# A fused S4D convolution and linear attention: softmax scaled on one sign, spectrum blocks permuted, the plan's priorities and engine leanings renumbered

## The chip, the cores and the metric

The kernel runs on one core of a Trainium2 chip. Its time is the device time of one execution in microseconds; of several executions the median is given. One execution is taken by the hardware profiler, and all rows of the trace come from that one. Engines are named as in the profile: PE (TensorE), DVE (VectorE), ACT (ScalarE), POOL (GpSimd), SP (SyncE, whose queue issues the DMAs).

## The reference

Two independent halves are computed from different inputs and concatenated along the last axis. L = S = 2048 positions, D = 576 channels, 32 heads of 18.

```python
# A: S4D long convolution, 128 states per channel
dt = exp(log_dt); A = -exp(log_A_real) + 1j * A_imag
C = (C_real + 1j * C_imag) * dt[:, None]
P = exp((A * dt[:, None])[:, :, None] * arange(L))
K = 2.0 * einsum("dn,dnl->dl", C, P).real
y = irfft(rfft(u.T, 2L) * rfft(K, 2L), 2L)[:, :L].T + u * D_skip

# B: linear attention with a learned feature map, per head
q, k, v = x @ wqkv
phi_q = concat(softmax(q @ w_phi), softmax(-(q @ w_phi)))   # 36 features
phi_k = concat(softmax(k @ w_phi), softmax(-(k @ w_phi)))
kv = phi_k.T @ v;  z = sum_s phi_k
o = (phi_q @ kv) / (phi_q @ z + 1e-6)
b = o.reshape(S, D) @ wo
```

## The kernel before

The program is written as some thousands of operations with a cost each, and a planner (`Plan.run`) puts them in order for all five engines before anything is emitted. An operation belongs to a numbered unit of a stage (`pl.at("query", 5)`), and a table `WANT` holds one due time for each unit. At every step the planner looks, on each engine, at the operations whose inputs and buffers are free and takes the one with the earliest start, and among those that could start within 100 ns of the engine's end the one with the smallest due time. TensorE pays a penalty `STAY` in that order for a change of its tile mode, ScalarE 1300 ns for a change of its activation table. An operation with two possible engines (an eviction from PSUM: ScalarE or VectorE; a sum of two tiles in SBUF: GpSimd or VectorE) goes where the planner expects it to end first. Where TensorE is expected to wait before a fresh PSUM buffer, the planner puts filler matmuls on a tile of zeros (`emit`, line 202), which keep the clock up. Nothing is reordered on the chip: each engine goes through its list and waits on semaphores.

The stages are:

- *fold*, *key* (16 tiles of 128 positions): w_phi is multiplied into the key weights (line 462 loads them); a tile of x is split into two fp32r parts, `xh` and `xl`, and multiplied with both parts of the weights, 42 matmuls a tile; then the softmax, and a matmul that adds to `kvt`.
- *softmax* (line 526 on): per head the largest and the smallest value (533, 534), the values less the largest (`e[:, 0]`), smallest less largest (`rg`), and rg less `e[:, 0]` for the other sign, one exponential over both signs (541), the sums over a head's 18 (542, 64 sums), a reciprocal (543), and one multiplication of all 1152 values.
- *query* (16 tiles): the same gemm and softmax, transposes of `e` to `fT` (618), matmuls with `kvb` that give numerator and denominator, division (634, 635), transposes of the result (645, 646), the output gemm, the store of `ot`.
- *u* (16 units): the first half of the transform of u, stored to `ud` in DRAM in 64 blocks.
- *mags*, *par* (6 blocks), *group* (36): the filter's powers. Six blocks of parameters; for each group GpSimd builds integer phases by doubling (824), ScalarE takes sines (833 to 835) and exponentials (854), VectorE multiplies them (859 to 864), TensorE sums over the states. *kfirst* (4) transforms the filter and stores it to `kd`.
- *product* (16): a product takes four blocks of u's transform and their mirror images (`block`, `take`, four to five DMAs `ub<-dram`), transforms them, multiplies with the filter's blocks (`ac`, 8 multiplications; then two differences and two sums of 128x288, `ac<-ac`), transforms back and stores `zo` to `zd` in six DMAs (`put`). *last* (16 units) reads `zd`, does the last transform and stores.

The mirror image of block q lies in block 64 - q, so a product's upper blocks stand in falling order and one at a time; `place` and `block` sort them out.

## Time and profile before

| what | value |
|---|---|
| executions shown | 649.92, 646.87, 649.16 us; median 649.16 |
| the profiled execution | 647.51 us, of which the span is 645.7 |
| granted TensorE clock, mean | 0.982 |
| DMA | 104.03 MB, mean 161 GB/s, 55.8% of sixteen engines' time |

In 40 equal slices of the span, the busy tenths of each engine, and the DMA share, are:

```profile
PE   8999999999999878988999989889999999998996
...
DVE  6899999999999879998799999879997889698762
ACT  4599599987867978697959598759945333235331
POOL 0355556445415363471362463425200001010000
```

A digit is the busy share of one slice of 16 us, 9 being 90% or more. TensorE's rows hold the fillers too. ScalarE and GpSimd are busy in the first three quarters, where the filter is built, and little in the last.

### The profile page before, as it was taken

What the parts mean: (1) busy time and instruction counts of PE and PEld (TensorE: products, weight loads), DVE (VectorE), ACT (ScalarE), POOL (GpSimd) and SP (SyncE); (2) the same over time, 40 slices, a digit from 0 to 9 for tenths busy, and PEclk for the clock granted to TensorE, in tenths of its full rate; (3) what the DMA queues carried; (4) which work ended last, traced back from release to release, by engine and by line L of the source; (5) the groups of instructions that cost most, each with busy time, mean ns of one, the idle gap of its engine ahead of it and who ended that gap; (6) DMA issues with size and microseconds to landing.
All of it is one profiled execution on the core that took longest, in us unless ns stands there. A gap on an engine that the chain in (4) does not pass through costs nothing.

```text
span 645.7 us, 19223 instructions
## 1 busy us (share of the span) xinstructions
PE 593.6 (92%) x7774; PEld 467.2 (72%) x7774; DVE 567.4 (88%) x1211; ACT 431.5 (67%) x704; POOL 213.0 (33%) x362
## 2 busy tenths in 40 slices
PE   8999999999999878988999989889999999998996
PEld 5878878887877756866766655665776867776885
DVE  6899999999999879998799999879997889698762
ACT  4599599987867978697959598759945333235331
POOL 0355556445415363471362463425200001010000
PEclk9999999999999978979999899999999999999999
DMA  8668543241036212137665686786476877875575
GB/s 217 199 220 265 149 136 125 90 123 46 22 87 181 68 41 65 36 82 201 204 180 144 171 222 162 193 235 175 132 249 168 249 221 227 243 210 151 161 226 166
DMA packets 101662, 104.03 MB, mean 161 GB/s; under 512 B 12358, under 2 KB 90054, under 8 KB 101574
## 3 DMA queue, kind: packets, MB, share of 16 engines
q1 hardware_dynamic: 101574, 102.81, 55.8%
q8 instruction: 61, 1.00, 0.7%
q14 instruction: 27, 0.22, 0.1%
HBM read 63.63 MB, written 39.06 MB: 159 GB/s over the span
## 4 chain that ended last, share of the span: by engine, by line
PE 36%; DVE 36%; ACT 10%; DMA 7%; issue 5%; SPq 4%; POOL 1%; POOLq 0%; DVEq 0%; ACTq 0%
PE ps L408 32%; DVE E L860 4%; DVE cs L859 4%; DVE e L422 4%; DVE small L542 3%; DVE E L862 2%; PE ps L618 2%; DVE E L864 2%; DVE ac L426 2%; DVE small L533 2%; DMA xi<-in_xT_dram 2%; DVE small L534 2%; SPq L596 2%; PE ps L202 1%; ACT ps L854 1%
## 5 line engine op out<-in xcount | busy, mean ns | idle before, releaser
L408 PE MATMUL ps<-wh,xl 128*128 128x288 f32 (+2 forms) x448 | 140.7, 314 | 1.3 <-DVE xl L422 1.0
L408 PE MATMUL ps<-wh,xh 128*128 128x378 f32 (+2 forms) x400 | 133.7, 334 | 1.4 <-ACT zi L413 0.8
L408 PE MATMUL ps<-wl,xh 128*128 128x378 f32 (+2 forms) x400 | 128.3, 321 | 0.0
L824 POOL TENSOR_TENSOR cs<-cs,pi 128x32 int32<-128x32 int32 (+4 forms) x180 | 114.8, 638 | 12.8
L408 PEld LDWEIGHTS ps<-wh,xl 128*128 128x128 f32 x448 | 84.3, 188 | 2.4 <-DVE xl L422 1.6
L408 PEld LDWEIGHTS ps<-wh,xh 128*128 128x128 f32 x400 | 75.3, 188 | 10.0 <-issue 2.3
L408 PEld LDWEIGHTS ps<-wl,xh 128*128 128x128 f32 x400 | 75.3, 188 | 0.0
L408 PE MATMUL ps<-E,cs 128*32 128x64 f32 x2304 | 46.1, 229 | 18.5 <-DVE E L862 12.9
L202 PE MATMUL ps<-zero 128*32 128x256 bf16 (+10 forms) x310 | 56.5, 318 | 4.1 <-DVE E L860 1.4
L408 PEld LDWEIGHTS ps<-E,cs 128*32 128x32 f32 x2304 | 37.2, 115 | 31.5 <-DVE E L862 16.7
L854 ACT ACTIVATE ps<-ps 128x512 f32<-128x512 f32 x108 | 56.7, 584 | 4.3 <-PE ps L408 3.9
L426 DVE TENSOR_TENSOR ac<-us,ps 128x288 f32<-128x288 f32 x128 | 49.9, 441 | 2.6 <-PE ps L408 2.5
L422 POOL TENSOR_TENSOR xh<-xi,xh 64x128 fp32r<-64x128 f32 x21 | 11.5, 547 | 120.2 <-DVE small L543 60.9
L819 POOL MEMSET cs<- 128x16 f32 x36 | 4.8, 133 | 138.9 <-PE ps L408 108.4
L859 DVE TENSOR_TENSOR cs<-ps,cs 128x1024 f32<-128x1024 f32 x36 | 43.7, 1215 | 7.2 <-ACT ps L854 7.0
L202 PEld LDWEIGHTS <-zero 128*128 128x128 bf16 (+6 forms) x310 | 30.1, 105 | 26.2 <-issue 15.4
L541 ACT ACTIVATE e<-e 128x1152 f32<-128x1152 f32 x32 | 37.1, 1168 | 17.8 <-DVE e L422 16.5
L542 DVE TENSOR_REDUCE small<-e 128x64 f32<-128x1152 f32 x32 | 42.7, 1342 | 6.8 <-ACT e L541 6.8
L408 PE MATMUL ps<-wh,xi 128*128 128x288 f32 x160 | 48.6, 306 | 0.0
L422 POOL TENSOR_TENSOR xl<-xi,xh 128x512 fp32r<-128x512 f32 x19 | 24.6, 1297 | 67.4 <-ACT xh L416 67.4
L408 PE MATMUL ps<-wl,xi 128*128 128x288 f32 x160 | 46.8, 295 | 0.0
L860 DVE TENSOR_TENSOR E<-ps,cs 128x1024 f32<-128x1024 f32 x36 | 43.4, 1204 | 0.0
(141 smaller groups left out, 1373.8 us busy)
## 6 DMA issues: line engine op xcount, KB each, us to landing
xi<-in_xT_dram SPq DMA_DIRECT2D x32, 320.0 KB
dram<-zi SPq DMA_DIRECT2D x16, 576.0 KB
dram<-zi SPq DMA_DIRECT2D x32, 288.0 KB
kb<-dram SPq DMA_DIRECT2D x32, 288.0 KB
zi<-dram SPq DMA_DIRECT2D x16, 576.0 KB
ub<-dram SPq DMA_DIRECT2D x62, 144.0 KB
ub<-in_u_dram SPq DMA_DIRECT2D x16, 288.0 KB
out_dram<-ot SPq DMA_DIRECT2D x16, 288.0 KB
```

The source lines that it names most:

```text
L202: self.matmul(t[0:cols, 0:n], self.zero.t[0:rows, 0:cols], self.zero.t[0:rows, 0:n])
L408: pe.matmul(o, l, r, start=start, stop=stop, skip_group_check=skip)
L422: op(eng, [c_dve(n) if e == "dve" else c_pool(n) for e in eng], lambda e: (dve if e == "dve" else pool).tensor_tensor(dst(), a(), b(), op= ...
L426: op(eng, c_dve(n) if eng == "dve" else c_pool(n), lambda: e.tensor_tensor(dst(), a(), b(), op=alu), r=r, w=w, lock=eng == "pool" or not a ...
L533: op("dve", c_dve(DH * m), lambda: dve.tensor_reduce(mx.t, v(), axis=AX.X, op=ALU.max), r=[p], w=[mx])
L534: op("dve", c_dve(DH * m), lambda: dve.tensor_reduce(mn.t, v(), axis=AX.X, op=ALU.min), r=[p], w=[mn])
L541: op("act", c_act(1152), lambda: act.activation(e.t, e.t, AF.Exp), r=[e], w=[e], table="exp")
L542: op("dve", 1270, lambda: dve.tensor_reduce(sm.t, e.t, axis=AX.X, op=ALU.add), r=[e], w=[sm])
L824: op("pool", c_pool(2 * n * W), lambda n=n, j=j: pool.tensor_tensor(x()[:, :, :, n:2 * n], x()[:, :, :, 0:n], pi.t[:, j:j + 2, gs].bitcast ...
L854: op("act", c_act(512), lambda p=p: act.activation(p.t, p.t, AF.Exp), r=[p], w=[p], table="exp")
L859: op("dve", c_dve(64 * W), lambda: dve.tensor_tensor(F(), both(M.t), F(), op=ALU.mult), r=[M, cs], w=[cs])
L860: op("dve", c_dve(64 * W), lambda: dve.tensor_tensor(E.t[:, :, :, 32:64], both(up.t), cs.t[:, :, :, 0:32], op=ALU.mult), r=[up, cs], w=[E])
```

## The change

**Softmax.** The maximum is taken negated (`negate=True`), so that maximum and minimum of a head lie side by side in one tile of pairs, and smallest less largest becomes a sum over pairs, a reduction with one input. For a query tile only the second sign is scaled, by (sum of the first sign) / (sum of the second); the factor common to both signs then cancels in the division, and the 1e-6 is multiplied by the first sign's sums (`total`). Key tiles keep the full scaling.

**Spectrum blocks.** The constants `f1` and `f2` are permuted, so that the four blocks of a product and their four mirror images each stand together. `take`, `put`, `place` and `block` go; a product loads `ub` in two DMAs of 128 partitions and stores `zo` in two. The tables `fu` and `fi` become one, `ff`.

**The plan.** A new table `LEAD` gives each named part of a stage (`pl.step`) an offset to its due time. `LEAN_ACT` and `LEAN_POOL` are added to VectorE's expected end where an operation may go to it or to ScalarE, or to it or to GpSimd: the first is -488 ns, the second +413. `STAY`, the 100 ns of the choice (`NEAR`) and all of `WANT` have new values, and a few costs are raised.

**Buffers.** `tmp` and `at` of the parameters share the buffers of `dt` and `ax`, `total` is new with three, and `small` has 8 buffers, not 12.

```diff
+    q = np.arange(32)
+    at = q // 4 * 4 + q % 2 * 2 + q // 2 % 2
+    q = np.concatenate([q, (64 - q)[1:], [32]])
+    at = np.concatenate([at, 32 + at[1:], [32]])
+    row = np.zeros(128, int)
+    for r in range(2):
+        row[2 * at + r] = 2 * q + r
+    f1, f2 = f1[:, row], f2[row]
...
+    def step(self, name):
+        self.part = name
...
-        self.ops.append([eng, cost, fn, deps, bufs, self.now - early, table, busy, lock and eng, (self.unit, early), mode, fill[0] if fill else None, alt])
+        self.ops.append([eng, cost, fn, deps, bufs, self.now - early - LEAD.get(self.part, 0.0), table, busy, lock and eng, (self.unit, early, self.part), mode, fill[0] if fill else None, alt])
...
-                        s = first(e, t, ops[k][8])
+                        s, late = first(e, t, ops[k][8]), 0.0
                         if e == "act" and ops[k][6] and table and ops[k][6] != table:
-                            s += 1300.0
+                            s, late = s + 1300.0, TURNOVER
...
+                            lean = LEAN_ACT if "act" in (e, x if main else ops[k][0]) else LEAN_POOL
+                            a, b = a + lean * (e == "dve"), b + lean * (e != "dve")
...
-                        key = (s if s > at[e] + 100.0 else at[e], ops[k][5] + (STAY if e == "pe" and ops[k][10] != mode else 0.0), k)
+                        key = (s + late if s + late > at[e] + NEAR else at[e], ops[k][5] + (STAY if e == "pe" and ops[k][10] != mode else 0.0), k)
...
-STAY = 4.0
+STAY, TURNOVER, NEAR, LEAN_POOL, LEAN_ACT = 39.6166, 43.0853, 13.9405, 412.6640, -488.3109
...
-            mx, mn = B("small", [128, m]), B("small", [128, m])
-            op("dve", c_dve(DH * m), lambda: dve.tensor_reduce(mx.t, v(), axis=AX.X, op=ALU.max), r=[p], w=[mx])
-            op("dve", c_dve(DH * m), lambda: dve.tensor_reduce(mn.t, v(), axis=AX.X, op=ALU.min), r=[p], w=[mn])
-            tt("dve", lambda: e.t[:, 0, hs, :], v, lambda: mx.t[:, :, None].to_broadcast([128, m, DH]), ALU.subtract, [p, mx], [e], DH * m)
-            tt("dve", lambda: rg.t[:, hs], lambda: mn.t, lambda: mx.t, ALU.subtract, [mn, mx], [rg], m)
+            ends = B("small", [128, m, 2])
+            op("dve", c_dve(DH * m), lambda: dve.tensor_reduce(ends.t[:, :, 0], v(), axis=AX.X, op=ALU.max, negate=True), r=[p], w=[ends])
+            op("dve", c_dve(DH * m), lambda: dve.tensor_reduce(ends.t[:, :, 1], v(), axis=AX.X, op=ALU.min), r=[p], w=[ends])
+            tt("dve", lambda: e.t[:, 0, hs, :], v, lambda: ends.t[:, :, 0:1].to_broadcast([128, m, DH]), ALU.add, [p, ends], [e], DH * m)
+            op("dve", c_dve(2 * m), lambda: dve.tensor_reduce(rg.t[:, hs], ends.t, axis=AX.X, op=ALU.add), r=[ends], w=[rg])
...
+        both = B("small", [128, 32, 2])
+        op("dve", c_dve(32), lambda: dve.tensor_copy(both.t[:, :, 0], sm.t[:, :, 0]), r=[sm], w=[both], lock=True)
+        op("dve", 270, lambda: dve.reciprocal(both.t[:, :, 1], sm.t[:, :, 1]), r=[sm], w=[both])
+        op("dve", c_dve(64), lambda: dve.tensor_reduce(rg.t, both.t, axis=AX.X, op=ALU.mult), r=[both], w=[rg])
+        tt(("pool", "dve"), lambda: e.t[:, 1], lambda: e.t[:, 1], lambda: rg.t[:, :, None].to_broadcast([128, H, DH]), ALU.mult, [e, rg], [e], 576)
...
+            op("dve", c_dve(n), lambda: dve.scalar_tensor_tensor(
+                den.t[:, :n], sm.t[:, h0:h0 + n, 0], 1e-6, pn.t[:, :n, 18], op0=ALU.mult, op1=ALU.add), r=[pn, sm], w=[den])
...
+        ff = B("ff", [128, 512])
+        op("sp", c_dma(128 * 2048), lambda: sp.dma_start(ff.t, i["ff"][p]), r=[ud], w=[ff])
...
+        four = lambda z, par: z.t[32 * par + 4 * p:32 * par + 4 * p + 4].rearrange("(j r) s d -> (r s) j d", r=2)
         for par in range(2):
-            for r in range(2):
-                put(par, r)
+            op("sp", c_dma(128 * 2304, 1152), lambda par=par: sp.dma_start(four(zd[half], par), zo[par].t), r=[zo[par]], w=[zd[half]])
```

The new numbers move instructions on every engine. Three places show how. The first is the start of SyncE's list of DMAs, before:

```order
L757 DMA dt<-in_ldt_dram 128x96
L759 DMA th<-in_aim_dram 128x96
L759 DMA cre<-in_cre_dram 128x96
L759 DMA cim<-in_cim_dram 128x96
L458 DMA fT<-in_wphi_dram 128x630
L462 DMA e<-in_wkT_dram 126x640 x3
L462 DMA E<-in_wkT_dram 126x640
L462 DMA kvb<-in_wkT_dram 72x640
L449 DMA xi<-in_xT_dram 128x5x128
L449 DMA zi<-in_wv_dram 128x5x192 x2
```

and after (`wkT` is the key weight in five blocks, `wv` the value weight in three, `xT` a tile of x, `u` a tile of u):

```order
L716 DMA ub<-in_u_dram 128x576
L463 DMA zi<-in_wv_dram 128x5x192
L463 DMA e<-in_wv_dram 128x5x192
L472 DMA fT<-in_wphi_dram 128x630
L476 DMA e<-in_wkT_dram 126x640 x2
L476 DMA E<-in_wkT_dram 126x640
L476 DMA kvb<-in_wkT_dram 72x640
L791 DMA dt<-in_ldt_dram 128x96
L793 DMA th<-in_aim_dram 128x96
L793 DMA cre<-in_cre_dram 128x96
L793 DMA cim<-in_cim_dram 128x96
L463 DMA xi<-in_xT_dram 128x5x128
```

The first u tile and two thirds of wv moved to the front, and the parameters behind the key weights; the fifth block of the key weights stands four loads after the last row shown, and the last third of wv after the first two stores `gd<-cs` of the magnitudes.

The second place is VectorE's list in one of the last products, between its multiplications `ac<-us,ps` and what follows, before:

```order
L426 TENSOR_TENSOR ac<-us_8022,ps 128x288 x4
L426 TENSOR_TENSOR ac<-us_8023,ps 128x288
L422 TENSOR_TENSOR ac<-ac 128x288
L426 TENSOR_TENSOR ac<-us_8023,ps 128x288
L422 TENSOR_TENSOR ac<-ac 128x288
L426 TENSOR_TENSOR ac<-us_8023,ps 128x288 x2
L426 TENSOR_TENSOR small<-small 128x16
L422 TENSOR_TENSOR ac<-ac 128x288
L422 TENSOR_TENSOR e<-small,e 128x576
L422 TENSOR_TENSOR ac<-ac 128x288
```

and after:

```order
L440 TENSOR_TENSOR ac<-us_7933,ps 128x288 x4
L440 TENSOR_TENSOR ac<-us_7934,ps 128x288 x4
L547 TENSOR_REDUCE small<-ps 128x16
L436 TENSOR_TENSOR ac<-ac 128x288
L548 TENSOR_REDUCE small<-ps 128x16
L557 TENSOR_REDUCE total<-e 128x2x32
L440 TENSOR_TENSOR e<-ps,small 128x288
L427 COPY us_8122<-ps 128x288
```

One of the four sums and differences is left on VectorE. The others stand in the last rows of GpSimd's list after the change, which held four `ac<-ac` in all before:

```order
L436 TENSOR_TENSOR xl<-xi,xh 128x512
L436 TENSOR_TENSOR xh<-xi,xh 64x128
L436 TENSOR_TENSOR ac<-ac 128x288 x3
L436 TENSOR_TENSOR e<-e,small 128x576
L436 TENSOR_TENSOR ac<-ac 128x288 x17
L436 TENSOR_TENSOR xh<-xi,xh 64x128 x2
```

The third place is SyncE's list around one of the later products, before:

```order
L922 DMA fi<-in_fi_dram 128x256
L1005 DMA dram<-zo 64x2x288 x2
L1008 DMA dram<-zo 64x288 x4
L922 DMA fu<-in_fu_dram 128x256
L939 DMA ub<-dram 64x2x288 x4
L968 DMA kb<-dram 128x2x288
L966 DMA fk<-in_fk_dram 128x256
```

and after:

```order
L967 DMA ub<-dram 128x2x288 x2
L960 DMA ff<-in_ff_dram 128x512
L1026 DMA dram<-zo 128x2x288 x2
L990 DMA kb<-dram 128x2x288
L988 DMA fk<-in_fk_dram 128x256
```

Six stores and four loads of 64 partitions became two and two of 128, and the loads of the next product stand ahead of the stores of the one before.

More of the change, by code (lines that the diff above doesn't have):

```diff
@@ new lines @@
+    ident=[-39.703],
+    fold=[-3814.5703, -4514.447, 174.1103, 544.6624],
+    start=[726.2842],
+    key=[-2909.7917, -0.0799, 220.563, 157.8162, -225.5153, 173.04, -1241.6879, -109.3988, -338.4576, -175.3779,
+          -2318.8196, 176.0873, 249.8555, 251.9596, -231.4053, 99.8816],
+    kv=[85.5267],
+    query=[476.857, 1690.9897, 4431.7125, 751.3041, 2777.2337, 589.8585, 3194.9953, 2789.5574, 367.711, 1380.6418,
+          914.5124, 1423.5053, 2499.5972, 1377.3193, 2733.1361, 817.2673],
+    u=[-102.8226, -226.0234, -1433.3706, -445.0721, -485.8874, -1597.2828, 880.8324, -734.4783, 728.5016, 739.4667,
+          -177.0395, 249.377, -557.77, 773.8434, 166.2647, -5869.6701],
@@ L387 @@
+    kfirst=[-2069.12, -388.4536, -152.51, 676.399],
+    product=[580.2793, 583.4571, 524.945, 1019.1475, 645.2543, 381.769, 375.2706, 687.6813, 2038.1628, 2418.0025,
+          2088.0002, 1103.4417, 2475.9162, 1427.038, 1252.1902, 1625.8165],
+    last=[326.0515, 549.9183, 360.8347, 614.2391, 1189.7141, 171.5588, 558.2575, -103.0095, 1111.1706, 1441.7724,
+          1346.2631, 1230.7698, 2479.1252, 3727.1339, 1655.5831, 3612.5906],
 )
@@ L399, in tags @@
                 pl.tag(t, p, n, window)
[L401 to L402 removed]
+    tags({1: "zero ident w1 w3 hp dsk kvb fT wh wl ks E sel dt th cre cim ax ay mx mn fx ld ldc",
+          2: "xi xh xl v1 o ot pi mg ff ub kb zo us2 ac yo zi", 3: "e fk total", 4: "cs", 8: "small"})
     tags({8: "ps"}, space=PSUM, window=1000)
@@ L539, in softmax @@
         tt(("pool", "dve"), lambda: e.t[:, 1], lambda: rg.t[:, :, None].to_broadcast([128, H, DH]), lambda: e.t[:, 0],
-           ALU.subtract, [rg, e], [e], 540)
-        op("act", c_act(1152), lambda: act.activation(e.t, e.t, AF.Exp), r=[e], w=[e], table="exp")
-        op("dve", 1270, lambda: dve.tensor_reduce(sm.t, e.t, axis=AX.X, op=ALU.add), r=[e], w=[sm])
-        op("dve", 470, lambda: dve.reciprocal(sm.t, sm.t), r=[sm], w=[sm])
-        tt(eng, lambda: e.t, lambda: e.t, lambda: sm.t[:, :, :, None].to_broadcast([128, 2, H, DH]), ALU.mult, [e, sm], [e],
-           1100)
+           ALU.subtract, [rg, e], [e], 576)
+        op("act", c_act(1152) + 40, lambda: act.activation(e.t, e.t, AF.Exp), r=[e], w=[e], table="exp")
+        pl.step("q2" if total else "k2")
+        op("dve", 1270, lambda: dve.tensor_reduce(sm.t.rearrange("p h s -> p s h"), e.t, axis=AX.X, op=ALU.add), r=[e], w=[sm])
+        if not total:
+            op("dve", 470, lambda: dve.reciprocal(sm.t, sm.t), r=[sm], w=[sm])
+            tt(FLEX, lambda: e.t, lambda: e.t, lambda: sm.t.rearrange("p h s -> p s h")[:, :, :, None].to_broadcast([128, 2, H, DH]),
+               ALU.mult, [e, sm], [e], 1100)
+            return e
+        both = B("small", [128, 32, 2])
[3 more added lines that the diff above has]
+        tt(("pool", "dve"), lambda: e.t[:, 1], lambda: e.t[:, 1], lambda: rg.t[:, :, None].to_broadcast([128, H, DH]), ALU.mult, [e, rg], [e], 576)
         return e
@@ L607, in query_tile @@
         ps = gemm_halves(load_x(t), wqo, have_q, 0)
-        e = softmax([(ps[c], slice(16 * c, 16 * c + 16), lambda c=c: ps[c].t.rearrange("p (h f) -> p h f", f=DH)) for c in range(2)], FLEX)
+        pl.step("q1")
+        sm = B("total", [128, 32, 2])
+        e = softmax([(ps[c], slice(16 * c, 16 * c + 16), lambda c=c: ps[c].t.rearrange("p (h f) -> p h f", f=DH)) for c in range(2)], sm)
+        pl.step("q3")
         fT = B("fT", [126, 10, 128])
@@ L830, in waves @@
     def waves(cs):
+        pl.step("g1")
         def f():
@@ L999, in product @@
             copy("any", lambda c=c, j=j, par=par: zo[par].t[:, j], lambda c=c: pz[c].t, [pz[c]], [zo[par]], HD)
-        def put(par, r):
-            q = 4 * p + 2 * r
-            s = lambda: zo[par].t[64 * r:64 * r + 64]
-            if not par:
-                op("sp", c_dma(64 * 2304, 1152), lambda: sp.dma_start(zd[half].t[q:q + 2].rearrange("j s d -> s j d"), s()), r=[zo[0]], w=[zd[half]])
-            else:
-                for j in range(2):
-                    op("sp", c_dma(64 * 1152, 1152), lambda j=j: sp.dma_start(block(1, 2 * r + j, zd[half]), s()[:, j]), r=[zo[1]], w=[zd[half]])
         for par in range(2):
-            for r in range(2):
-                put(par, r)
+            op("sp", c_dma(128 * 2304, 1152), lambda par=par: sp.dma_start(four(zd[half], par), zo[par].t), r=[zo[par]], w=[zd[half]])
     for half in range(2):
```

105 lines of the change are left out of this document (44 added, 61 removed).

## The prediction

> **What bounds the kernel now.** I read the page's engine totals first, then its chain, then the busy time of each engine by stretch.
>
> ```profile
> span 645.7 us, 19223 instructions
> ...
> PE 593.6 (92%) x7774; PEld 467.2 (72%) x7774; DVE 567.4 (88%) x1211; ACT 431.5 (67%) x704; POOL 213.0 (33%) x362
> ...
> PE 36%; DVE 36%; ACT 10%; DMA 7%; issue 5%; SPq 4%; POOL 1%; POOLq 0%; DVEq 0%; ACTq 0%
> ```
>
> No one engine owns the end: PE and DVE have equal shares of the chain of waits. An average over the span hides which of them leads where, so I cut the span at three events: 40 us (the start is over), 224 us (VectorE has done the 13th of 36 filter groups) and 484 us (it has done the 36th; from here on there are only query tiles, products and last stages). The columns are the stretch, its length, then busy time and count of PE, PEld, DVE, ACT and POOL, the granted clock, the DMA share and GB/s. The second table is the same for the filler matmuls (L202), which the plan puts where it expects TensorE to wait.
>
> ```profile
> 0.00:40.00 40.00, 36.31 (x270) 29.22 (x271) 31.00 (x79) 24.50 (x45) 11.77 (x24) 1.00 0.69 196
> 40.00:224.00 184.00, 173.10 (x2636) 149.02 (x2637) 179.17 (x348) 153.49 (x226) 87.63 (x155) 1.00 0.42 124
> 224.00:484.00 260.00, 233.26 (x3329) 173.07 (x3324) 237.64 (x493) 196.93 (x309) 106.54 (x178) 0.96 0.56 157
> 484.00:645.70 161.70, 150.97 (x1552) 115.90 (x1550) 119.58 (x294) 56.59 (x126) 7.07 (x6) 0.99 0.71 202
> ```
>
> ```profile
> 0.00:40.00 40.00, 9.78 (x42) 4.27 (x42) 1.00 0.69 196
> 40.00:224.00 184.00, 5.82 (x32) 2.78 (x32) 1.00 0.42 124
> 224.00:484.00 260.00, 28.62 (x174) 16.48 (x174) 0.96 0.56 157
> 484.00:645.70 161.70, 12.30 (x62) 6.62 (x62) 0.99 0.71 202
> ```
>
> Two regimes stand there. Up to 484 us **VectorE** leads: it is idle 9.0, 4.8 and 22.4 us in the three stretches, while TensorE without fillers does 26.5, 167.3 and 204.6 us of work. After 484 us **TensorE** leads: 138.7 us of work and 12.3 of fillers in 161.7 us, VectorE idle for 42.1 and GpSimd nearly unused. So the change is worth what it does to VectorE's work and waits in the first 484 us, and to TensorE's work and waits in the last 162.
>
> **Work that changes engine.** These are the groups behind the sum (count, busy us, mean ns of one, idle time before).
>
> ```profile
> L422 DVE TENSOR_TENSOR e<-e,small 128x1152 f32<-128x1152 f32 x27 | 37.7, 1403 | 0.2
> L422 DVE TENSOR_TENSOR ac<-ac 128x288 f32<-128x288 f32 x60 | 28.7, 497 | 0.0
> L413 DVE COPY zi<-ps 128x288 f32<-128x288 f32 x58 | 23.4, 447 | 2.8 <-PE ps L408 2.7
> L422 DVE TENSOR_TENSOR e<-small,e 128x576 f32<-128x576 f32 x27 | 21.4, 791 | 0.2
> L543 DVE RECIPROCAL small<-small 128x64 f32<-128x64 f32 x32 | 17.3, 543 | 0.2
> L422 DVE TENSOR_TENSOR xl<-xi,xh 128x512 fp32r<-128x512 f32 x13 | 9.6, 739 | 2.5 <-ACT xh L416 2.5
> L413 DVE COPY ks<-ps 128x256 f32<-128x256 f32 x13 | 5.4, 416 | 1.0 <-PE ps L408 0.8
> L635 DVE RECIPROCAL small<-small 128x21 f32<-128x21 f32 x16 | 4.6, 287 | 0.3
> L422 DVE TENSOR_TENSOR xh<-xi,xh 64x128 fp32r<-64x128 f32 x11 | 4.4, 401 | 0.3
> L413 DVE COPY fT<-ps 126x512 f32<-126x512 f32 x5 | 3.4, 683 | 0.5 <-PE ps L618 0.5
> ...
> L634 DVE TENSOR_SCALAR small<-ps 128x21 f32<-128x21 f32 x16 | 2.8, 174 | 4.5 <-PE ps L408 4.2
> ```
>
> ```profile
> L422 POOL TENSOR_TENSOR e<-small,e 128x576 f32<-128x576 f32 x5 | 5.8, 1166 | 9.9 <-DVE small L426 9.9
> L422 POOL TENSOR_TENSOR ac<-ac 128x288 f32<-128x288 f32 x4 | 3.5, 897 | 3.0 <-DVE ac L426 3.0
> ```
>
> The counts come from the two programs' orders. On VectorE:
> - The sums and differences of a product (ac from ac) fall from 60 to 9: 51 x 497 ns = -25.3 us. GpSimd takes them at 897: +45.7.
> - A query tile's division scales 576 elements, not 1152. Of the multiplications 14 of 1152 are left (from 27) and 10 of 576 are new: -13 x 1403 + 10 x 791 = -10.3 us. The differences of 576 fall from 27 to 19: -6.3.
> - The splits of x move to GpSimd: 11 of xh and 3 of xl, -4.4 - 2.2 = -6.6 us.
> - Sixteen reciprocals of 64 become 16 of 32. The trace has no such one; it lies between 287 ns (21) and 543 (64), and I take 350 by length: -3.1 us. Each of these tiles gains a copy of 32 and a product-reduction of 64. The nearest row, 174 ns for 21 elements, bounds them below, and the reciprocal of 64 above; I take 185 each, since neither holds much data: +5.9 us, at most +17.
> - Evictions from PSUM go the other way. ScalarE gives up 102: 14 of 512 columns at 683, 14 of 256 at 416, the rest about 288 at 447, less two that return: +48.6 us on VectorE, and some -43 on ScalarE.
> - The 1e-6 of the denominator is one instruction before and after; 174 ns, and I take no difference.
>
> That is +2.8 us before one more item. The key and query tiles subtract minimum and maximum per head, 64 times, with two inputs in SBUF:
>
> ```profile
> L426 DVE TENSOR_TENSOR small<-small 128x16 f32<-128x16 f32 (+2 forms) x64 | 17.2, 274 | 0.1
> ```
>
> ```profile
> 601.35 0.16 DVE L426 TENSOR_TENSOR small<-small 128x16 f32<-128x16 f32 x1
> ...
> 604.07 0.76 DVE L422 TENSOR_TENSOR e<-small,e 128x576 f32<-128x576 f32 x1
> ```
>
> Late, with GpSimd idle, one takes 160 ns, where the mean is 274 (the difference of 576 takes 0.76 us there, 791 ns in the mean). The sum over pairs that replaces it has one input. At 170 ns it saves 64 x 104 = 6.7 us; if the stretch only passes to the next instruction, nothing. I take 6. **VectorE's total then falls by about 3 us**, GpSimd's rises by 45.7, by 14 instructions of 576 at 1166 ns (16.3, less three of 1152 that go) and by the 14 splits, some 65 in all, to 43% of the span. ScalarE loses 43 and gains three table loads, off the bound. Nearly all of VectorE's 3 us lies in the tail, where it does not lead: in the first 484 us its load is unchanged. This change cannot pay through VectorE's load; it must pay through waits.
>
> **Waits in the middle.** TensorE's fillers are where the plan leaves it waiting. By the orders there are 74 before the 13th group's matmuls, then 174, then 62; after the change 133, 89 and 51. In the third stretch a filler takes 28.62 us / 174 = 164 ns, so 85 fewer are 14 us less of TensorE waiting for VectorE's products. VectorE leads there, so I read its idle time: 22.4 us, shrunk in the same ratio (89/174), is 11.4. **I take -11 us**; the ends are 0 (fillers are a plan, not a measurement) and -14.
>
> **Start.** The other direction: 59 more fillers before the 13th group, at (9.78 + 5.82) / 74 = 211 ns, are 12.4 us. The cause is SyncE's order: a u tile and two thirds of wv now stand ahead of the folded key weights, and the last third of wv stands behind the stores of the filter magnitudes. Before, it went:
>
> ```profile
> 7.97 4.10 PE L408 MATMUL ps<-fT,e 126*128 126x126 f32 x30 [1.52 <-DMA e<-in_wkT_dram]
> ...
> 15.13 0.46 PE L408 MATMUL ps<-wh,xh 128*128 128x378 f32 x1
> ```
>
> ```profile
> 27.07 0.36 DVE L533 TENSOR_REDUCE small<-ps 128x11 f32<-128x198 f32 x1 [0.63 <-PE ps L408]
> ```
>
> The first key gemm starts at 15.1 us and the first half-tile that needs all of wv reaches VectorE at 27.1. But VectorE leads here, and the new order puts more of its other work (parameters of a second block, magnitudes, u evictions) ahead of that instruction: 76 rows against 52, 9 us more by the row means. That work hides the later gemm; without it all 12.4 us would show. I take **+4 us**, ends 0 and +12.4.
>
> **Tail.** Fillers fall from 62 to 51: 11 x 12.30 / 62 = -2.2 us. Work leaves it for the first 484 us, where TensorE has room: one query gemm half and a bit (18 matmuls), ten of the output gemm, 16 of the last stage and five transposes, each some 0.13 us at the spacing of the trace, -6 us. Against it, GpSimd now adds the products before the inverse transform: 26 times 897 - 497 = 0.4 us, two in a row, so 1.6 us a product if nothing covers it. Gemms of other tiles do, mostly; I take +2 (of at most 10). **Tail -6 us**, ends -9 and +4.
>
> **Merged transfers.** Stores of zo fall from 96 to 32, loads of ub from 66 to 32, fu and fi become one. SyncE issues them without a pause late in the kernel:
>
> ```profile
> 562.89 1.27 SPq L1005 DMA_DIRECT2D dram<-zo  x2
> 564.26 2.81 SPq L1008 DMA_DIRECT2D dram<-zo  x4
> 567.17 0.53 SPq L922 DMA_DIRECT2D fu<-in_fu_dram  x1
> 567.74 2.58 SPq L939 DMA_DIRECT2D ub<-dram  x4
> ```
>
> ```profile
> 529.06 1.19 PE L408 MATMUL ps<-ub,fu 64*32 64x288 f32 x26 [0.98 <-DMA ub<-dram]
> ```
>
> That is some 7 us of issue a product, and it would be under 3. But between 500 and 600 us this 0.98 us is one of two waits of TensorE that the trace shows: gemms hide the queue. I take 0, and down to -4 if the queue also holds back the loads behind it.
>
> **Sum.** 0 + 4 - 11 - 6 + 0 = -13 us. The profiled execution took 647.51 (645.7 of span); the median shown is 649.16, 0.25% above it. By the median that is **636 us**.
>
> **Rivals.**
> *A bigger gain (0.18).* ScalarE, 43 us lighter, answers VectorE sooner, and both ends are good: 0 at the start, -14, -9, -4 = -27, so 622. For it: a tenth of the chain is ScalarE. Against: VectorE waited on it for few us.
> *No change (0.17).* VectorE keeps its idle time in the middle, since its load there is the same: 0 + 4 + 0 - 6 = -2, 647.
> *Slower through the start (0.14).* The first tiles lack wv, VectorE runs out of parameter work, and what stood behind stays as late: +12.4 - 2 = +10, so 659. It decides when VectorE's idle time in the first 40 us passes 9.0 by more than the 11 us won in the middle.
> *Slower through GpSimd (0.09).* Two-input VectorE work and GpSimd get in each other's way:
>
> ```profile
> 5.05 0.25 DVE L426 TENSOR_TENSOR mn<-ax,ay 128x96 f32<-128x96 f32 x1
> ...
> 144.82 1.34 DVE L426 TENSOR_TENSOR mn<-ax,ay 128x96 f32<-128x96 f32 x1
> ```
>
> ```profile
> 144.69 1.35 POOL L422 TENSOR_TENSOR xl<-xi,xh 128x512 fp32r<-128x512 f32 x1 [3.32 <-ACT xh L416]
> ```
>
> The same instruction takes 0.25 us alone and 1.34 beside GpSimd's, ending just after it. Some 60 large two-input instructions are left on VectorE; if a third of them stood 1 us, that is 20, less the 13: +7, so 656. But the difference of 576 took 0.76 us alone and 791 ns in the mean, so the mean stretch was small, and VectorE loses more such instructions than it keeps. The Trainium skill ("SBUF — State Buffer", section "Who interferes with whom") says that a VectorE instruction with two SBUF inputs and a GpSimd instruction that reads SBUF exclude each other for a whole instruction, whichever starts first; the trace agrees (0.25 against 1.34 us). By it GpSimd's 51 new additions can also wait for VectorE.
>
> **How the numbers follow.** Forecast 0.42, the rivals as given. Faster or slower means by over 0.5% of 649, about what a measurement of this kernel can tell from no change. Faster: the forecast, the bigger gain and a little more, 0.61; same: 0.19; slower: 0.20. The range runs from just below the bigger gain, 619, to 656: the slow start at its full price is left out, and little of the low side.
>
> **What would show it.** Right: VectorE's total within 10 us of 567, ScalarE near 391, GpSimd near 278, VectorE's idle time between the 13th and 36th group near 11, the last stretch near 156. Wrong: VectorE idle well over 9 us in the first 40 (the start), TensorE waiting for ac from GpSimd late in the kernel (the additions), or stretched VectorE instructions in the group region (the shared access).

## The result, and the profile after

The changed kernel takes **624.09 us** (median of 4; 622.21 to 626.59) beside 648.01 us (645.06 to 649.92) of the kernel before: a ratio of 0.9637, 95% interval 0.9584 to 0.969, so 24 us less. The profiled execution took 622.21 us, 620.4 of it span, at a granted clock of 0.979 (before 0.982). One execution below, the profiled one of e1, was disturbed (3155 us, the others 685 to 686), and no row of it is read. First the page's engine totals and its chain, of the changed kernel:

```profile
span 620.4 us, 19048 instructions
...
PE 588.6 (95%) x7734; PEld 462.5 (75%) x7737; DVE 557.9 (90%) x1269; ACT 401.1 (65%) x605; POOL 269.1 (43%) x438
...
PE 59%; DVE 21%; ACT 9%; DMA 6%; issue 3%; SPq 1%; DVEq 0%; ACTq 0%
```

Then the busy time by stretch, cut at the same events as before (40 us, VectorE's 13th filter group at 233.2, its 36th at 471.7; the columns are those of the prediction's table), and the fillers (L213 now) in the same stretches:

```profile
0.00:40.00 40.00, 35.83 (x200) 24.02 (x201) 28.07 (x68) 22.15 (x38) 16.25 (x34) 1.00 0.82 238
40.00:233.20 193.20, 185.60 (x2768) 164.63 (x2766) 185.84 (x387) 148.36 (x196) 105.11 (x163) 0.98 0.32 90
233.20:471.70 238.50, 225.19 (x3279) 165.32 (x3282) 227.70 (x513) 190.64 (x290) 117.89 (x206) 0.96 0.65 194
471.70:620.40 148.70, 141.98 (x1491) 108.53 (x1490) 116.26 (x304) 39.92 (x83) 29.81 (x37) 0.99 0.68 207
```

```profile
0.00:40.00 40.00, 19.63 (x91) 9.34 (x91) 1.00 0.82 238
40.00:233.20 193.20, 5.73 (x42) 3.87 (x42) 0.98 0.32 90
233.20:471.70 238.50, 15.64 (x87) 7.47 (x89) 0.96 0.65 194
471.70:620.40 148.70, 10.55 (x50) 5.27 (x51) 0.99 0.68 207
```

Read beside the table of before, the 25.3 us of span come out like this:

| stretch | length before, after | VectorE's busy time | VectorE's idle time | TensorE's idle time |
|---|---|---|---|---|
| to the 13th group | 224.0, 233.2 (+9.2) | +3.7 | 13.8 to 19.3 | 14.6 to 11.8 |
| 13th to 36th group | 260.0, 238.5 (-21.5) | -9.9 | 22.4 to 10.8 | 26.7 to 13.3 |
| after the 36th | 161.7, 148.7 (-13.0) | -3.3 | 42.1 to 32.4 | 10.7 to 6.7 |

The kernel starts more slowly, as feared, and makes up for it more than three times (34.5 us against 9.2). The chain has moved as well: TensorE has 59% of it and VectorE 21%, where they shared it evenly before.

### The profile page after: what moved, and what is told of

Its sections match the earlier page's. It is cut to its first block, busy times and chain, and to the rows that moved or that the text cites. A ratio compares the mean times of both kernels' runs of the same rounds, so it can differ in the third digit from the quotient of the medians.

```text
span 620.4 us, 19048 instructions
## 1 busy us (share of the span) xinstructions
PE 588.6 (95%) x7734; PEld 462.5 (75%) x7737; DVE 557.9 (90%) x1269; ACT 401.1 (65%) x605; POOL 269.1 (43%) x438
## 4 chain that ended last, share of the span: by engine, by line
PE 59%; DVE 21%; ACT 9%; DMA 6%; issue 3%; SPq 1%; DVEq 0%; ACTq 0%
PE ps L422 55%; DVE ac L440 3%; PE ps L646 2%; DVE E L898 2%; DVE cs L897 2%; DVE total L557 2%; DMA dt<-in_ldt_dram 2%; DMA dram<-zi 1%; ACT cs L870 1%; ACT cs L868 1%; DVE E L902 1%; ACT cs L869 1%; DVE E L900 1%; PE ps L213 1%; ACT ps L891 1%
## 5 line engine op out<-in xcount | busy, mean ns | idle before, releaser
L422 PE MATMUL ps<-wh,xl 128*128 128x288 f32 (+2 forms) x448 | 141.5, 316 | 0.6 <-DVE xl L436 0.5
L858 POOL TENSOR_TENSOR cs<-cs,pi 128x512 int32<-128x512 int32 (+4 forms) x180 | 115.2, 644 | 10.1
L436 POOL TENSOR_TENSOR ac<-ac 128x288 f32<-128x288 f32 x55 | 43.3, 808 | 41.8 <-DVE ac L440 32.3
L436 POOL TENSOR_TENSOR xl<-xi,xh 128x512 fp32r<-128x512 f32 x22 | 31.2, 1417 | 64.1 <-PE ps L422 30.1
L213 PE MATMUL ps<-zero 128*32 128x256 bf16 (+11 forms) x270 | 51.5, 327 | 3.2 <-DVE zero L456 1.2
L440 DVE TENSOR_TENSOR ac<-us,ps 128x288 f32<-128x288 f32 x128 | 48.6, 444 | 1.7 <-issue 0.9
L422 PE MATMUL ps<-E,cs 128*32 128x64 f32 x2304 | 42.7, 224 | 7.2 <-DVE E L900 4.6
L422 PEld LDWEIGHTS ps<-E,cs 128*32 128x32 f32 x2304 | 35.2, 111 | 18.5 <-DVE E L900 7.1
L512 ACT ACTIVATE xh<-xi 128x640 fp32r<-128x640 f32 x32 | 23.6, 738 | 36.5 <-DMA xi<-in_xT_dram 23.7
L422 PEld LDWEIGHTS ps<-kvb,fT 126*128 126x128 f32 (+1 forms) x320 | 38.2, 189 | 8.5 <-issue 2.1
L213 PEld LDWEIGHTS <-zero 128*128 128x128 bf16 (+6 forms) x273 | 25.9, 103 | 23.8 <-issue 12.1
```

What stands on the lines that cost most here:

```text
L213: self.matmul(t[0:cols, 0:n], self.zero.t[0:rows, 0:cols], self.zero.t[0:rows, 0:n])
L422: pe.matmul(o, l, r, start=start, stop=stop, skip_group_check=skip)
L436: op(eng, [c_dve(n) if e == "dve" else c_pool(n) for e in eng], lambda e: (dve if e == "dve" else pool).tensor_tensor(dst(), a(), b(), op= ...
L440: op(eng, c_dve(n) if eng == "dve" else c_pool(n), lambda: e.tensor_tensor(dst(), a(), b(), op=alu), r=r, w=w, lock=eng == "pool" or not a ...
L512: op("act", c_act(640) + 40, lambda: act.activation(xh.t, xi.t, AF.Copy), r=[xi], w=[xh])
L858: op("pool", c_pool(2 * n * W), lambda n=n, j=j: pool.tensor_tensor(x()[:, :, :, n:2 * n], x()[:, :, :, 0:n], pi.t[:, j:j + 2, gs].bitcast ...
```

## The experiments

Most of them keep the order in which the changed kernel's plan puts the instructions and change only what is emitted at one place, so that one part stands alone. Only the first two let the plan run anew. Each was timed beside runs of the kernel before; the last column is (its ratio - 0.9637) x 648 us, its distance from the changed kernel.

| run | median us | ratio to before, interval | from the changed kernel |
|---|---|---|---|
| e1_new_ops_old_numbers | 686.14 | 1.0561, 1.0496 to 1.0626 | +60 |
| e2_old_ops_new_numbers | 687.65 | 1.0587, 1.0530 to 1.0644 | +62 |
| e3_transfers_in_halves | 635.35 | 0.9771, 0.9713 to 0.9829 | +8.7 |
| e4_sums_on_dve | 638.91 | 0.9823, 0.9758 to 0.9889 | +12 |
| e5_issue_only | 654.41 | 1.0065, 1.0023 to 1.0108 | +28 |
| e6_query_scaled_in_full | 629.73 | 0.9675, 0.9629 to 0.9720 | +2.5 |
| e7_evictions_to_act | 625.55 | 0.9597, 0.9535 to 0.9659 | -2.6 |
| e8_difference_of_two | 622.92 | 0.9570, 0.9522 to 0.9618 | -4.3 |
| e9_halves_on_two_queues | 647.38 | 0.9990, 0.9955 to 1.0025 | +23 |
| e10_no_low_times_high | 612.19 | 0.9467, 0.9399 to 0.9534 | -11 |
| e11_no_fillers | 630.91 | 0.9745, 0.9695 to 0.9795 | +7.0 |
| e12_less_of_both | 613.09 | 0.9437, 0.9377 to 0.9498 | -13 |

The changed kernel's own interval is 3.4 us to either side, so e6, e7 and e8 can't be told from it.

### Operations and numbers apart

e1 keeps the new operations and gives the plan its old numbers; e2 keeps the old operations and gives it the new ones (without a few of the raised costs). The lines of the diff are e1's; `LEAD` is emptied, and `WANT` gets its old values.

```diff
-STAY, TURNOVER, NEAR, LEAN_POOL, LEAN_ACT = 39.6166, 43.0853, 13.9405, 412.6640, -488.3109
+STAY, TURNOVER, NEAR, LEAN_POOL, LEAN_ACT = 4.0, 0.0, 100.0, 0.0, 0.0
+LEAD = dict()
```

> The changed operations (softmax, merged transfers, buffers) under the numbers of before: its table of due times, no offsets, no leanings, the old penalties. Theory (the gain is in the order that the new numbers set, not in the operations): the plan has 406 fillers here against 273 after the change and 310 before, so the gain goes and the time is 640 to 660 us. Rival (the operations themselves bring it: less work in the query softmax, fewer stretched subtractions, merged transfers): 625 to 635.

> The operations of before (full scaling of the query softmax, subtraction of maximum from minimum, four blocks loaded and stored apart) under all numbers of the change. Theory (order): most of the gain stays, 628 to 642 us, with GpSimd again near 270 us and ScalarE near 400. Rival (operations): the gain goes, 642 to 652.

Both took 686 to 688 us, some 37 us more than even the kernel before, which no expectation allowed. In e2, cut at the same events, all three stretches are longer: 257.1, 266.0 and 163.0 us, where the changed kernel has 233.2, 238.5 and 148.7. The numbers fit one set of operations, and either mixture is worse than either pair. So the gain can't be split between operations and numbers; what can be asked is what each part is worth in the order that the change ends up with.

### The merged transfers

In e3 each load of `ub` is two DMAs of 64 partitions again, and the stores of `zo` are two and four.

```diff
+        def load(par):
+            for h in range(2):
+                sp.dma_start(ub[par].t[64 * h:64 * h + 64], two(ud, par, h)[:, :, cs])
...
-sp.dma_start(ub[par].t, four(ud, par)[:, :, cs])
+load(par)
-sp.dma_start(four(zd[half], par), zo[par].t)
+store(par)
```

> The changed kernel with its order kept; only each load of ub is issued as two DMAs of 64 partitions, each store of zo as two (lower blocks) or four (mirror blocks) as before the change. Theory (the issue time on SyncE's queue lies beside gemms): 0 to 4 us slower, 624 to 628. Rival (the freed queue is what shortened the last stretch by 13 us): 632 or more, with waits of TensorE for ub and kb.

It took 8.7 us more by the ratios, and 14.0 by the two spans. The profiled execution of the changed kernel is the fastest of its four and that of e3 the slowest, so a difference of stretches is rather too large. The theory (0 to 4 us) is missed; the time is in the range of the rival, but the waits of TensorE for ub and kb that went with it did not come: those for ub are not listed, those for kb are 2.8 us in all (1.5 in the changed kernel). The last two stretches of its profile hold nearly all of the difference (13.3 us):

```profile
233.90:479.00 245.10, 227.51 (x3279) 165.46 (x3282) 227.76 (x513) 190.46 (x290) 117.59 (x206) 0.97 0.65 186
479.00:634.40 155.40, 145.15 (x1491) 110.43 (x1490) 117.53 (x304) 39.54 (x83) 30.61 (x37) 0.98 0.71 198
```

VectorE's work in the middle is the same to 0.1 us (227.76, 227.70), and its idle time is 17.3 us, not 10.8. For a measure of how far stretches scatter: in e6 and e8 below, whose transfers stay merged, the middle takes 239.9 and 238.5 us with 10.3 and 9.6 idle, the tail 153.1 and 150.1. So the loss in the middle stands clear of other differences; that in the tail hardly does. It goes with a change in SyncE's queue. The timeline of the changed kernel's SyncE around one product (start, length, line, transfer, count), then that of e3 at the same place:

```profile
503.97 1.00 SPq L967 DMA_DIRECT2D ub<-dram  x2
506.35 0.35 SPq L960 DMA_DIRECT2D ff<-in_ff_dram  x1
506.97 0.87 SPq L1026 DMA_DIRECT2D dram<-zo  x2
509.35 0.36 SPq L990 DMA_DIRECT2D kb<-dram  x1
```

```profile
511.93 2.57 SPq L970 DMA_DIRECT2D ub<-dram  x4
514.59 0.54 SPq L960 DMA_DIRECT2D ff<-in_ff_dram  x1
515.23 2.41 SPq L978 DMA_DIRECT2D dram<-zo  x4
517.73 1.26 SPq L975 DMA_DIRECT2D dram<-zo  x2
519.09 1.13 SPq L1003 DMA_DIRECT2D kb<-dram  x1
```

The four merged transfers keep SyncE for 1.9 us, the ten halves for 6.2, and the pauses in which SyncE was ready for the next load are gone. Added up over the DMA instructions alone, without the waits between them, SyncE issues for 297.4 us in the kernel before (502 issues), 205.5 in the changed one (388) and 282.6 in e3 (484). Who waits for a late load is told by the waits: ScalarE, which splits each tile of x, in the changed kernel and in e3 (total, times, longest):

```profile
ACT xh L512 <- DMA xi<-in_xT_dram: 23.7, 11, 8.0
```

```profile
ACT xh L512 <- DMA xi<-in_xT_dram: 40.5, 13, 7.9
```

e5 tried to put back issue time alone: six DMAs of 64 bytes a product, from DRAM to DRAM, behind those that were merged.

```diff
+    def more(n):
+        for _ in range(n):
+            extra[0] += 1
+            t = junk.tile([1, 16], F32, name=f"junk{extra[0]}", tag=f"junk{extra[0]}")
+            sp.dma_start(t, i["fk"][0][0:1, 0:16])
```

> The changed kernel with its order kept; each product issues six more DMAs on SyncE's queue, one after each load of ub, one after the first and three after the second store of zo, each of 64 bytes from one DRAM tensor to another, so that the number of issues is that of e3 but the transfers stay whole. Theory (e3's 11 us come from the time that SyncE's queue spends on issues, which holds back the loads of x behind it): 630 to 637 us, with ScalarE's waits for x near e3's 40 us. Rival (they come from the transfers of 64 partitions themselves): 622 to 627.

That was worse than either expected, +28 us. ScalarE's wait for x is 50.9 us, more than e3's, as the theory would have it; but SyncE's issue time, 267.6 us, is below e3's 282.6, so issue time alone doesn't set the price. The DMA engines' share of the hardware queue (packets, MB, share of sixteen engines) is, in the changed kernel, e3 and e5:

```profile
q1 hardware_dynamic: 97702, 102.80, 55.6%
```

```profile
q1 hardware_dynamic: 99238, 102.81, 56.8%
```

```profile
q1 hardware_dynamic: 100774, 102.81, 60.1%
```

96 added DMAs of 64 bytes made 3072 packets and took 0.601 x 16 x 649.4 - 0.556 x 16 x 620.4 = about 725 us of engine time; the 96 halves of e3, by the same sum, 1536 packets and 246 us. The small ones were no clean stand-in for issue time.

e9 is e3 with the 96 added issues on ScalarE's queue.

```diff
-sp.dma_start(ub[par].t[64 * h:64 * h + 64], two(ud, par, h)[:, :, cs])
+(act if h else sp).dma_start(ub[par].t[64 * h:64 * h + 64], two(ud, par, h)[:, :, cs])
-sp.dma_start(two(zd[half], par, h)[:, j], zo[par].t[64 * h:64 * h + 64, j])
+(act if h or j else sp).dma_start(two(zd[half], par, h)[:, j], zo[par].t[64 * h:64 * h + 64, j])
```

> The changed kernel with its order kept and the merged transfers taken apart again as in e3_transfers_in_halves (635.35 us), but the added 96 issues go through ScalarE's queue, so that SyncE issues as few as in the changed kernel (394, 279.9 us of issue time there against 352.7 us in e3). Theory: SyncE's issue time in its in-order queue made e3 slow, so the time goes back to 622 to 629 us. Rival: the form of the transfers (64 partitions each) or their number on the DMA engines made it slow: 632 to 640 us. Above 640 us ScalarE's own waits at the added issues would have cost more than either, and nothing is told.

It took 647.38 us, above the 640 from which it tells nothing of the question. (The 279.9 and 352.7 us of its expectation were added up from timeline rows, which hold waits between issues; the issues alone take the 205.5 and 282.6 us given above, and there are 388 of them in the changed kernel, not 394.) But its waits are worth reading:

```profile
ACT xh L512 <- DMA xi<-in_xT_dram: 24.1, 8, 8.1
...
DVE cs L897 <- ACT ps L891: 14.1, 10, 4.9
ACT xi L430 <- DMA dram<-zo: 14.0, 4, 4.3
```

ScalarE's wait for x is back at the changed kernel's value (24.1, 23.7 us), with SyncE's queue nearly as short as there (212.9 us of issues). In its place stand ScalarE's own delays behind the added issues, which take 67.3 us of its queue (96 issues, 0.70 us each), and VectorE's wait for ScalarE (14.1 us, 3.3 in the changed kernel). That fits SyncE's queue as the cause of the late x. It doesn't prove it, since a ScalarE that comes later itself waits less. Nor is it shown that the late x is what costs the time: of the chain that ended last, transfers of x hold 5.8 us in the changed kernel and 9.8 in e3, but 12.2 in e4 below, whose transfers are merged. What the issue time costs apart from the form of the transfers stays open.

### The sums on GpSimd, the query's scaling, the difference

e4 emits all 64 sums and differences of a product on VectorE, at their places in the order.

```diff
-        o[2](eng) if o[12] else o[2]()
+        o[2]("dve" if o[9][2] == "p3" else eng) if o[12] else o[2]()
```

> The changed kernel with its order kept; only all sums and differences of a product (64 of 128x288) are emitted on VectorE, 55 of them taken from GpSimd. Theory (VectorE leads up to the last group, TensorE after it): the 29 of them ahead of the last group cost VectorE 29 x 0.44 = 13 us, those behind it up to 5, so 8 to 16 us slower, 632 to 640. Rival (VectorE's load does not set the time, or GpSimd's slower sums hold up the inverse transforms): 0 to 4 us slower or faster, 618 to 628.

+12 us by the ratios, within the theory's 8 to 16. The last two stretches, and VectorE's group of these sums in e4:

```profile
234.40:486.90 252.50, 229.37 (x3280) 166.33 (x3282) 239.29 (x541) 191.17 (x290) 98.43 (x178) 0.97 0.62 183
486.90:639.20 152.30, 145.43 (x1491) 109.69 (x1490) 124.38 (x330) 39.90 (x83) 9.28 (x11) 1.00 0.68 202
```

```profile
L436 DVE TENSOR_TENSOR ac<-ac 128x288 f32<-128x288 f32 x64 | 31.5, 498 | 0.1
```

In the middle VectorE has 11.6 us more work, and the stretch is 14.0 longer; in the tail 8.1 us more work cost 3.6. The spans differ by 18.8 us where the ratios give 12 (the profiled execution of e4 is its slowest), so in the middle what is put on VectorE is paid mostly, perhaps in full.

e6 scales both signs of a query tile again, with a reciprocal of 64 and no copy and product-reduction.

```diff
-        tt(("pool", "dve"), lambda: e.t[:, 1], lambda: e.t[:, 1], lambda: rg.t[:, :, None].to_broadcast([128, H, DH]), ALU.mult, [e, rg], [e], 576)
+        op(("pool", "dve"), [c_pool(576), c_dve(576)], lambda n: (dve if n == "dve" else pool).tensor_tensor(
+            e.t, e.t, both.t.rearrange("p h s -> p s h")[:, :, :, None].to_broadcast([128, 2, H, DH]), op=ALU.mult), r=[e, rg, both], w=[e], lock=True)
```

> The changed kernel with its order kept; the query softmax takes the reciprocal of all 64 sums, scales all 1152 values at the place where the change scales 576, and adds 1e-6 in the denominator, as before the change; copy and product-reduction are left out. Theory (VectorE loses little: 10 multiplications of 1152 for 576 there, 16 reciprocals of 64 for three small instructions, so +3 us of work, and 6 multiplications on GpSimd 0.9 us longer each): 1 to 5 us slower, 625 to 629. Rival (the scaling stands on the path of each query tile, 0.6 to 0.9 us each): 10 us or more slower, 634 or above.

+2.5 us by the ratios: the rival (10 us or more) is out, and the theory's 1 to 5 us can't be told from nothing. VectorE's busy time is 565.3 us, 7.4 more.

e8 writes the sum over pairs as an addition of two inputs again.

```diff
-dve.tensor_reduce(rg.t[:, hs], ends.t, axis=AX.X, op=ALU.add)
+dve.tensor_tensor(rg.t[:, hs], ends.t[:, :, 1], ends.t[:, :, 0], op=ALU.add)
```

> The changed kernel with its order kept; the 64 sums over pairs are two-input additions of the same numbers instead. Theory (a two-input instruction waits for GpSimd, 0.1 us each in the mean): 2 to 7 us slower, 626 to 631, and their mean near 0.27 us where the sum over pairs took 0.17. Rival (the wait only passes to the next instruction): within 1.5 us, 622.5 to 625.5.

No change (-4.3 us, within the intervals): the theory's 2 to 7 us more did not come, and the rival, that the wait only passes on, fits better. The instruction itself does get slower; the group in the changed kernel, then in e8:

```profile
L550 DVE TENSOR_REDUCE small<-small 128x16 f32<-128x32 f32 (+2 forms) x64 | 11.1, 174 | 0.0
```

```profile
L550 DVE TENSOR_TENSOR small<-small 128x16 f32<-128x16 f32 (+2 forms) x64 | 15.1, 235 | 0.0
```

4 us of VectorE's busy time come and go with no difference in the time that could be measured.

### What bounds the changed kernel

Three runs take load away. e7 hands 118 evictions from VectorE to ScalarE, where ScalarE is expected to end first by 100 ns; e10 leaves out, in `gemm`, the product of the low half of x with the high half of the weights; e12 does both.

```diff
+                            if "act" in (e, y):
+                                self.plain[k, e] = y if e == "dve" and b + MARGIN < a else e
```

```diff
-                mm(p, xl.t[:, k, :], wh.t[:, k, cs], False, False)
```

> The changed kernel with its order kept; 118 evictions that the leaning put on VectorE are emitted on ScalarE at the same place of the order, so that ScalarE has 295 of them (177 after the change, 279 before). Theory (the evictions wait on ScalarE behind sines, exponentials and table loads, so PSUM buffers come free late): 5 to 25 us slower, 629 to 649, although VectorE has 50 us less work. Rival (VectorE's load sets the time): 10 us or more faster, 614 or less.

> The changed kernel with its order kept; in gemm the product of the low half of x with the high half of the weights is left out: 320 matmuls of 316 ns mean, about 101 us of TensorE's 588.6 us, over all stretches. VectorE keeps its 557.9 us. Theory (TensorE, VectorE and the chain between them are all near their limit in the changed kernel): the time falls by 15 to 45 us, to 579 to 609 us, most of it in the last stretch, where TensorE has 142.0 us busy of 148.7 and VectorE 116.3. Rival 1 (TensorE alone is the bound): a fall of 70 us and more, to 554 us or less. Rival 2 (VectorE alone is the bound up to 472 us): only the last stretch falls, by up to 15 us, with the stretches before within 3 us of 233.2 and 238.5.

> The changed kernel with its order kept and both reliefs at once: the 118 evictions on ScalarE of e7_evictions_to_act (VectorE 517.7 us busy in place of 557.9; alone 625.55 us, no change) and the product of the low half of x with the high half of the weights left out as in e10_no_low_times_high (TensorE 539.8 us busy in place of 588.6; alone 612.19 us, 12 us less). Theory (TensorE and VectorE are both at the limit in the same stretches, each covering the other): both together give clearly more than the 12 us, 580 to 600 us. Rival (what is left is the chain of waits, transfers and SyncE's queue, and neither engine's load sets the time): 607 to 615 us, with PE and VectorE both under 88% busy.

e7 is as fast as the changed kernel with 40.2 us less on VectorE: neither expectation held. VectorE's idle time rises from 62.5 to 100.4 us, and the largest of its waits is for ScalarE, 15.0 us where the changed kernel has 3.3:

```profile
DVE cs L902 <- ACT ps L896: 15.0, 17, 3.0
```

e10 gains 11 us where TensorE's busy time falls by 48.8, less than its theory had, and not in the last stretch alone, as its second rival had it. (All 448 such matmuls went, not the 320 that the expectation counted.) Its page and its last two stretches:

```profile
PE 539.8 (88%) x7289; PEld 403.2 (66%) x7289; DVE 556.8 (91%) x1269; ACT 398.8 (65%) x605; POOL 269.1 (44%) x438
...
DVE 51%; PE 21%; ACT 13%; DMA 8%; issue 5%; SPq 1%; POOL 1%; DVEq 0%; ACTq 0%; POOLq 0%
```

```profile
230.10:464.10 234.00, 212.60 (x3165) 149.45 (x3165) 226.47 (x513) 189.26 (x290) 117.78 (x207) 0.97 0.66 199
464.10:611.10 147.00, 131.69 (x1366) 94.63 (x1366) 116.05 (x305) 39.78 (x83) 30.41 (x37) 0.97 0.69 210
```

The chain goes over from TensorE (59%) to VectorE (51%), and the last stretch, which TensorE was said to lead, falls by 1.7 us only, with 10.3 less of TensorE's work in it. e12, with both reliefs, is no faster than e10, so its rival held:

```profile
PE 534.4 (87%) x7286; PEld 400.1 (65%) x7289; DVE 520.0 (85%) x1151; ACT 435.0 (71%) x723; POOL 270.5 (44%) x438
...
DVE 35%; PE 25%; ACT 23%; DMA 10%; issue 5%; POOL 1%; SPq 1%; ACTq 0%; DVEq 0%; POOLq 0%
```

```profile
232.00:467.90 235.90, 210.02 (x3163) 147.59 (x3165) 210.19 (x463) 203.71 (x340) 118.51 (x206) 0.99 0.66 197
```

In its middle stretch TensorE and VectorE are each idle for some 26 us of 235.9 and ScalarE for 32, and the stretch is 2.6 us shorter. Work taken out of the order leaves idle time there; what sets the length of the stretch then isn't shown. That ScalarE, fuller in e7 and e12, has become a bound of its own is not excluded.

e11 leaves out the fillers.

```diff
-        if fill:
+        if False:
```

> The changed kernel with its order kept and its 270 filler matmuls (51.5 us) left out. Theory (fillers stand only where TensorE would have waited, and hold the granted clock): without them TensorE's idle time grows by about as much, the clock falls below 0.97 in the stretches, and the time rises by 3 to 25 us, to 627 to 649 us. Rival (fillers stand partly on the path, since TensorE is near the bound now): 612 to 622 us.

+7.0 us, as its theory had it, with the granted clock at 0.954 on the mean (0.979 with fillers). In the first 40 us it is lowest:

```profile
0.00:40.00 40.00, 20.66 (x108) 18.35 (x109) 24.57 (x62) 20.60 (x36) 14.19 (x30) 0.87 0.76 221
```

The 13th group is done at 238.3 us there, 5.1 later. TensorE's idle time grows from 31.8 to 68.3 us, by 36.5 of the 51.5 us that the fillers took. So fillers stand mostly where TensorE waits, as the prediction read them; whether the lower clock or the waits make the 7 us isn't told apart.

## Why the prediction came out as it did

It said 636 us (619 to 656), 13 us less than before, and the kernel lost 24. The direction and the range were right; three sizes were off, and one of them because a part was priced at nothing. That the sum came out within the range is in part luck: the start was worse than said, and the rest better.

**VectorE's load (-3 us): near as a total, wrong in its place.** Added up by count and mean, as the prediction did, VectorE's instructions take 645.2 us before and 645.7 after; its busy time, which counts overlapping instructions once, fell by 9.5 us. The single terms came out close:

```profile
L436 DVE TENSOR_TENSOR ac<-ac 128x288 f32<-128x288 f32 x9 | 6.2, 690 | 0.0
...
L565 DVE RECIPROCAL small<-total 128x32 f32<-128x32 f32 x16 | 5.4, 340 | 0.0
...
L566 DVE TENSOR_REDUCE small<-small 128x32 f32<-128x64 f32 x16 | 3.4, 211 | 0.1
L564 DVE COPY small<-total 128x32 f32<-128x32 f32 x16 | 2.9, 184 | 0.0
```

The reciprocal of 32 was taken at 350 ns and took 340; copy and product-reduction at 185 each took 184 and 211; the evictions added 47.6 us where 48.6 were forecast. What failed is the sentence that nearly all of it lies in the tail, with the load of the first 484 us unchanged: the middle stretch, which VectorE leads, lost 9.9 us of its busy time. The prediction concluded that the change cannot pay through VectorE's load. e4 speaks against it: with the sums back on VectorE, at the same order, the kernel loses 12 of the 24 us.

**The start (+4 us, ends 0 and +12.4): the right mechanism, undersized.** The first key gemm starts at 24.7 us, where it was 15.1, and the first half-tile that needs all of wv reaches VectorE at 44.3, where it was 27.1:

```profile
24.71 0.44 PE L422 MATMUL ps<-wh,xh 128*128 128x378 f32 x1 [0.35 <-ACT wh L487]
```

```profile
44.30 0.35 DVE L547 TENSOR_REDUCE small<-ps 128x11 f32<-128x198 f32 x1
```

Ahead of that instruction VectorE has 12.4 us more work (32.1, 19.7 before; forecast 9) and 4.8 us more idle time (12.2, 7.4 before), so most of the delay is covered, as said. But the 13th group came 9.2 us later: by then VectorE has idled 5.5 us more (2.9 of it in the first 40) and done 3.7 us more work. No run changed the order of the first loads alone, so that they are the cause is read from the trace alone.

**Waits in the middle (-11 us): right in size, in part by luck.** VectorE's idle time between the 13th and the 36th group was forecast to shrink from 22.4 to 11.4 us with the fillers; it is 10.8, and the fillers fell to 87, as the order said. Yet with the transfers taken apart again (e3), in the same order and with the same 87 fillers, it is 17.3: by these two traces some half of the 11.6 us hangs on the merged transfers, which the prediction had put at nothing.

**Merged transfers (0, down to -4 us): the step that failed.** That "gemms hide the queue" was read off TensorE's waits alone. In this order the merge is worth 8.7 us by the ratios, 14.0 by the profiled spans. By the spans 6.6 us fall in the middle stretch and 6.7 in the tail, and only the first is clear of the scatter between runs. The wait that grows most without it is ScalarE's for x, whose loads stand behind the halves; the path from there to the end isn't shown. Of the kernel before, the waits did show part of it, in rows that the prediction passed over:

```profile
PEld ps L408 <- DMA ub<-dram: 4.5, 8, 1.5
PE ps L408 <- DMA kb<-dram: 3.8, 3, 1.7
```

Between 500 and 600 us, where the prediction counted two waits of TensorE, five are above 0.15 us; the two longest are for SyncE's loads (`ub` 0.98 us, `kb` 0.94). In the changed kernel the first row is gone and the second is 0.6 us. The wait of ScalarE for x was 13.8 us then, less than the 23.7 of now, so the price is one in the new order; what the merge alone would have brought in the old one wasn't tried.

**The tail (-6 us): twice that, -13.0.** The fillers shrank by 1.75 us (forecast 2.2) and TensorE's other work by 7.3 (forecast 6). The sums on GpSimd were priced at +2; with them on VectorE (e4) the stretch is 3.6 us longer, not shorter, so nothing shows that they cost time there; nor that they save any, since in e6, whose sums stay on GpSimd, it is 4.4 longer. No wait of TensorE for GpSimd's sums is listed. The rest of the 13.0, 4.0 us, is TensorE's idle time (10.7 to 6.7); in e3 it is 10.2 again, but in e6, with the transfers merged, 10.5, so what lowered it stays open.

In sum: the start 5 us worse than said, the middle 10.5 better (its VectorE work), the tail 7 better, which makes -25 where -13 stood.

**The rivals.** *A bigger gain* came nearest in time (622 us) but not by its mechanism: e7 gives ScalarE its load back (437.0 us; 431.5 before) and is as fast. *No change* and *slower through the start* fell with the middle stretch. *Slower through GpSimd* showed only in traces: the nine sums left on VectorE take 690 ns in the mean, and all 64 take 498 in e4, where GpSimd has none of them. Of the nine, the two that no GpSimd instruction overlaps take 444 and 446 ns, the other seven 443 to 985. That agrees with the rule of the Trainium skill ("SBUF — State Buffer", "Who interferes with whom") which the prediction weighed. Nine times 0.19 us is only 1.7 us, and the differences of 576 on VectorE kept their length (781 ns; 791 before).

**The signs named ahead.** VectorE's total (557.9, within 10 of 567), ScalarE's (401, near 391), GpSimd's (269, near 278) and the idle time in the middle (10.8) came as said; the last stretch did not (148.7, said 156). VectorE's idle time in the first 40 us rose to 11.9, the mild form of the slow start.

**What stays open.** Taken back singly, the merged transfers cost 8.7 us and the sums on GpSimd 12; they were not taken back together, so whether the two make up most of the 24 us isn't shown, nor what the new order is worth by itself (e1 and e2 tell only that it doesn't fit other operations). Further open: the part of the merge that is SyncE's issue time, against the number and form of the transfers (e5 and e9 failed to separate them); and what holds the middle stretch at 236 us with load taken off both engines (e12). No run here is measurably faster than the changed kernel without leaving work out.

## What to carry to other kernels

Treat a queue that issues DMAs like an engine: add up its issue time by stretch (205.5 of 620.4 us here, after the merge), and before a merged transfer is priced at nothing, look for who waits for the loads that stand behind it, not only for who waits for the transfer itself. A tuned order and its numbers belong to one set of operations; to learn what one part is worth, keep the order and change only what is emitted there. When an engine at 90% is relieved and the time stays, the order and its waits may set the time, and adding to that engine may still cost most of what is added.
